# Output rows of the first block in runs of 64, one pool of two product banks, and longer planned landing times in a three-stage attention and MoE kernel

## The chip, the cores and the metric

One core of a Trainium2 chip runs the whole program: TensorE (PE) with its weight loads (PEld), VectorE (DVE), ScalarE (ACT), GpSimd (POOL) and SyncE (SP). All transfers between DRAM and SBUF are issued by SP, one after the other. The metric is the device time of one execution in microseconds, the median of several runs. TensorE's clock has two levels, 2.4 GHz (a granted clock of 1.00 in the profile) and 1.2 GHz (0.50).

## What is computed

Attention over chunks of 64 tokens, then a first network with squared ReLU, then a second one with a rational activation. All is fp32.

```python
def reference(**kwargs):                       # cut
    attn_out = _attn_ref(q, k, v)              # 8 x 8 heads, 576 tokens, head_dim 64, chunks of 64
    x = transpose(attn_out).reshape(4608, 512)
    x = _moe_ref(x, w_in, w_out)               # h = x @ w_in; r = max(h, 0); g = r*r; g @ w_out
    return _moe2_ref(x, w_in, w_out, a, b)     # d_ff = 2048 in both
def _moe2_ref(x, w_in, w_out, a, b):
    h = x @ w_in
    P = a[0] + a[1]*h + a[2]*h**2 + a[3]*h**3
    Q = 1.0 + abs(b[0])*abs(h) + abs(b[1])*h**2
    return (P / (Q + 1e-06)) @ w_out
```

## The kernel before, in words

The 4608 tokens are cut into nine blocks of 512 (NB), the 2048 hidden columns into 16 slices of 128 (NF). Each fp32 product is made of three matmuls on a high and a low part (`mm3`, L371 to L375); one such matmul of 512 columns is the unit of PE work, and twelve of them make one slice of a block.

**Stage 1** runs to about 825 us: network 1 (`mm_h` L381 for its first product, sums in the four banks `acc` for its second) with the attention of the next blocks in between. The first product of a slice goes to a PSUM bank `h`. ACT reads it with `act1` (L488, the ReLU; L489 squares it), DVE or ACT make the high part `gh`, POOL the low part `gl`. Two banks serve this, tags `h0` and `h1`, which `h_bank` (L377) hands out in turn; the same two banks also take the attention's products with v (`mm_pv2`, L582, matmul at L589; emptied by copies `ah<-h`, L199) and the transposes of the weights e (L766). A bank that was handed out can be written when the reader of its former content is through.

**Stage 2** runs from there to the end: network 2. Its first product is made for pairs of blocks by a scheme of seven products (p = 1 to 7) of six matmuls each, on sums of weights (`w2q`) and sums of x, in place of eight. A unit of this scheme (two slices, two blocks) is seven products and four jobs of the second product ("o"), about 20.4 us of PE; eight units make a block pair m = 0 to 3, so that the units are numbered 0 to 31, and the ninth block comes last. The banks are now four: `bank(i)` (L863), tags `h0`, `h1` and `b2`, `b3`, given to roles b, g, h, e of a unit by `role` (L867). The results wait there for `tile_jobs` (L1251): several operations by DVE, ACT and POOL (L922 to L970), the product `t` of POOL at L942 among them.

The sums of x for a pair are made on the side: `xq_load` (L336, DMA at L342) brings rows of x2 into a room `xroom`, `xq_sum` (L346) adds on POOL (L350), `xq_hi` (ACT) and `xq_lo` (POOL) split, `xq_store` (L362, DMA at L366) writes the pages `x2q`, which are loaded again as pages of x (L849) as the units need them. The output rows of a block leave by `store2` (L471, DMA at L476).

The order in stage 2 is set by `plan` (L1185), a list scheduler with costs and due times in units of one matmul (0.227 us). It keeps SP's queue in the order of planned starts. `X_LAT` (L1227) is how long it plans for the landing of a load of x, and also from the store of one sum to the load of the next but one into the same room. SP issues in order and can have eight transfers under way (eight semaphores in turn, DMAHW0 to DMAHW7 below): an instruction that waits holds up everything behind it on SP.

Of the kernel before, what the change touches and what calls it, by code (L numbers as in the profile page):

```python
# [9 lines left out]
F32 = mybir.dt.float32  # L10
# [6 lines left out]
PSUM = bass.MemoryType.PSUM  # L17
# [7 lines left out]
RING_O, RING_I, RING_X = 6, 12, 9  # L25
# [3 lines left out]
R_SB = "g"  # L29
MORE = 3  # L30
N_PRE = 2
TB = {"r": 3, "t": 3, "w": 3}
OF_W = {1: 0, 2: 2, 3: 7, 4: 3, 5: 4, 6: 5, 7: 6}
OF_X = {1: 0, 2: 1, 7: 2, 3: 3, 4: 4, 5: 5, 6: 6}
# [54 lines left out]
def attn_moe_moe_kernel(  # L89
# [25 lines left out]
    nc = tc.nc  # L115
    B, H, S, D = q.shape
# [4 lines left out]
    NF = DFF // 128  # L121
    NBLK = NT // NB
# [7 lines left out]
    g_p = ctx.enter_context(tc.tile_pool(name="g", bufs=3))  # L130
    r_p = ctx.enter_context(tc.tile_pool(name="r", bufs=1))
    dram_p = ctx.enter_context(tc.tile_pool(name="scr", bufs=1, space=DRAM))
    h_p = ctx.enter_context(tc.tile_pool(name="hps", bufs=1, space=PSUM))

    X = [[xs.tile([128, KC, NB], F32R, name=f"x{i}{p}") for p in range(2)] for i in range(2)]
    const = ctx.enter_context(tc.tile_pool(name="const", bufs=1))
# [22 lines left out]
    P = {}  # L159
    T = {}  # L160
# [214 lines left out]
            nc.tensor.matmul(out=o, lhsT=ah, rhs=bh, start=False, stop=last and i == len(pairs) - 1, **kw)  # L375

    def h_bank():  # L377
        T["h_n"] = T.get("h_n", 1) ^ 1
        return h_p.tile([128, 512], F32, name="h", tag=f"h{T['h_n']}")

    def mm_h(s):  # L381
        b, f = divmod(s, NF)
# [44 lines left out]
    def mm_out2(s, g):  # L427
        f = s % NF
        w = w_out(s)
        stage("out", s, 0)  # L430
        for i in range(TPB):
            gi = [x[:, i * 128:(i + 1) * 128] for x in g]
            if s < 2 * NS - 1 or i < TPB - 1:
                mm3(ACC[i], [(gi, w)], f == 0, s == 2 * NS - 2 and i == TPB - 1 or f == NF - 1)
                continue
            for j in PARTS:
                T["rest", j.start] = h_bank()
                mm3(T["rest", j.start][:, j], [(gi, [z[:, j] for z in w])], True, True)

    def g_tiles():  # L440
# [29 lines left out]

    def store2(b, i):  # L471
        t0 = b * NB + i * 128
        rows = out[t0:t0 + 128, :]
        if b == 0:
            rows = out[256 * (i // 2):256 * (i // 2) + 256, :].rearrange("(t c u) d -> c t u d", c=2, u=64)[i % 2]
        nc.sync.dma_start(out=rows, in_=T.pop(("ev", i)))  # L476

    def act1(s):
        ps = T.pop(("h", s))
# [381 lines left out]
        split_lo(nc.gpsimd, o[:, 1], o[:, 1].bitcast(F32), o[:, 0])  # L861

    def bank(i):  # L863
        i %= 4
        return h_p.tile([128, 512], F32, name="h", tag=f"h{i}") if i < 2 else P["eb"].tile([128, 512], F32, name="h", tag=f"b{i}")

    def role(un, r):  # L867
        if un == 0:
            return "bghe".index(r)
        if ("role", un, r) not in T:  # L870
            T["role", un, r] = role(un - 1, NEXT[r])
        return T["role", un, r]
# [212 lines left out]
    for t in range(NAT, NTILE + 1, 2):  # L1085
# [15 lines left out]
        u = (t - NAT) // 2  # L1101
# [79 lines left out]
    def job(eng, cost, deps, due, fn, *args):  # L1181
        jobs.append((eng, cost, deps, due, fn, args))
        return len(jobs) - 1
# [40 lines left out]
                    wait.setdefault(jobs[k][0], []).append(k)  # L1224
        return end

    E_LAT, PE_LAT, D_LAT, X_LAT = 0.6, 1.2, 13.0, 30.0  # L1227
    pe_list = []
    n_out = 0
    for m in range(NBLK // 2):  # L1230
# [50 lines left out]
    def x_jobs(i, deps):  # L1281
        m = i // 7
        if m < NBLK // 2 and ("xq", 8 * m + 7) not in made:
            later.setdefault(m, []).append((i, deps))
            return
        deps = deps + ([(made["xq", 8 * m + 7], D_LAT)] if m < NBLK // 2 else [(made["st", NBLK - 1, k], D_LAT) for k in range(KC)])
        due = nominal["p", m, 0, ORDER[i % 7]] if m < NBLK // 2 else nominal["s", 0]
        for c in range(2):
            made["x", i, c] = job("D", 6.5, deps, due - 40, xp_load, i, c)
# [6 lines left out]
    for x in pe_list:  # L1296
# [43 lines left out]
        if x[0] == "p":  # L1340
            _, m, u, p = x
            b1, b2, f0, f1 = 2 * m + 1, 2 * m, 2 * u, 2 * u + 1
            un, i = 8 * m + u, ORDER.index(p)
            j, i = 7 * un + i, 7 * m + i
            if ("i", j) in made:
                deps.append((made["i", j], D_LAT))
            if u == 0:
                deps += [(made["x", i, c], D_LAT) for c in range(2) if ("x", i, c) in made]
            if p in (1, 5):
                deps += last_of.get(role(un, "he"[p == 5]), [])  # L1350
            if p in (6, 2, 3, 7, 4):
                deps += [(made[k, un], E_LAT) for k in {6: ["fb"], 2: ["fb"], 3: ["v"], 7: ["v"], 4: ["add22"]}[p]]
            made[x] = job("PE", size["p"], deps, 0, mm_p, m, u, p)
            end = [(made[x], PE_LAT)]
            z = nominal[x]
            if j + RING_I < len(i_seq):
                i_job(j + RING_I, end)
            if u == NF // 2 - 1 and i + RING_X < 7 * (NBLK // 2) + 2:
                x_jobs(i + RING_X, end)
            if p == 1:  # L1360
                made["fb", un] = job("A", COST["cp"], end + last_of.get(role(un, "b"), []), z + 7, q_fork, un, "h", "b")
            if p == 5:
                q_ = [(made["add22", un - 1], E_LAT)] if un else []
                made["s5", un] = job("A", COST["cp"], end + q_, z + 8, q_s5)
            if p in (5, 6) and ORDER.index(p) == max(ORDER.index(5), ORDER.index(6)):
                made["v", un] = job("V", COST["add"], end + [(made["s5", un], E_LAT)], z + 8, q_v)
            if p == 2:
                last_of[role(un, "b")] = tile_jobs(b1, f0, end, z + 44, "b" not in R_SB)
            if p == 3:
                last_of[role(un, "e")] = tile_jobs(b2, f0, end, z + 44, "e" not in R_SB)  # L1370
            if p == 7:
                made["add22", un] = job("V", COST["add"], end + [(made["s5", un], E_LAT)] + last_of.get(role(un, "g"), []),
                                        z + 6, q_22, un, b2, f1)
                last_of[role(un, "g")] = tile_jobs(b2, f1, [(made["add22", un], E_LAT)], z + 44, "g" not in R_SB)
            if p == 4:
                last_of[role(un, "h")] = tile_jobs(b1, f1, end, z + 44, "h" not in R_SB)
            if u < 5 and p in (1, 7) and (u, p) != (0, 1) and m < NBLK // 2 - 1 and (m or u):
                i = 8 * m + 8 + 2 * u + (p == 7) - (1 if m else 2)
                if i < 8 * m + 16:
                    q_ = [(made["xq", i - 2], X_LAT)] if i > 9 else []  # L1380
                    e = job("D", 3, end + q_, z + 20, xq_load, i)
                    e = job("G", 10.5, [(e, X_LAT)], z + 60, xq_sum, i)
                    e = job("A", 4.3, [(e, E_LAT)], z + 75, xq_hi, i)
                    e = job("G", 10.5, [(e, E_LAT)], z + 100, xq_lo, i)
                    made["xq", i] = job("D", 11.5, [(e, E_LAT)], z + 140, xq_store, i)
                    if i == 8 * m + 15:
                        for i, q_ in later.pop(m + 1, []):
                            x_jobs(i, q_)
                        if m == 0:
                            for i in range(7, RING_X):  # L1390
                                x_jobs(i, end)
            continue
        f = x[1]
        u, i = divmod(f, 2)
# [85 lines left out]
```

## Time and profile before

| | us |
|---|---|
| median of 3 runs | 1625.17 (1623.68 to 1625.43) |
| the profiled execution | 1624.63 |
| its span, first to last instruction | 1622.9 |
| PE busy in it | 1593.5 (98%) |
| DVE, ACT, POOL busy | 1076.8, 920.5, 770.1 |
| mean granted clock of PE | 0.994 |

The profile is one execution. The sum of the prediction is made in that execution's times, and 1.7 us of it lie outside of the span. Since PE is busy 98% of the span, what matters is where it is not, and where its clock is low. The second section of the page, the span in 40 slices, has a slice in which PE falls to 7 tenths and its clock to 8: the 26th, from 1014 to 1055 us.

### The profile page before, as it was taken

Reading aid. Unit: us, or ns where it says so; the run is one execution under the profiler, and the core shown is the slowest. Engines: PE = TensorE matmul, PEld = TensorE weight load, DVE = VectorE, ACT = ScalarE, POOL = GpSimd, SP = SyncE. Lnnn points to the kernel's source line nnn. Section 1 sums busy time; section 2 is a strip of 40 time slices with the busy share of each in tenths; the row PEclk is TensorE's granted clock in tenths of the full one; section 3 lists DMA queues with packets and bytes.
Section 4 is the critical chain, followed back from the end, with each engine's and each line's share of the span. In section 5 each row is a group of like instructions: output and inputs, shape, how many; then the busy total and the mean of one; then the engine's idle time right before and its main releaser. Section 6 shows DMA issues by size and latency. Waiting matters only on the chain.

```text
span 1622.9 us, 25746 instructions
## 1 busy us (share of the span) xinstructions
PE 1593.5 (98%) x9165; PEld 1317.5 (81%) x9165; DVE 1076.8 (66%) x1688; ACT 920.5 (57%) x1462; POOL 770.1 (47%) x737
## 2 busy tenths in 40 slices
PE   8899999999999999999999999799999999999998
PEld 7778888888888888888888888688888888888887
DVE  6776676666666766653067887688788877777640
ACT  5754333333333332334578876787788778777641
POOL 3531122022221312323368864886598657555554
PEclk9999999999999999999999999899999999999999
DMA  9745575344445445544989995999999896666544
GB/s 264 215 106 137 158 239 130 86 140 107 128 115 142 119 101 144 143 124 132 318 304 296 307 346 205 305 301 304 343 292 298 299 349 213 205 210 210 179 161 138
DMA packets 359448, 337.29 MB, mean 208 GB/s; under 512 B 195352, under 2 KB 269336, under 8 KB 358296
## 3 DMA queue, kind: packets, MB, share of 16 engines
q1 hardware_dynamic: 359320, 335.64, 67.0%
q8 instruction: 73, 1.20, 0.3%
q14 instruction: 55, 0.45, 0.1%
HBM read 253.76 MB, written 81.79 MB: 207 GB/s over the span
## 4 chain that ended last, share of the span: by engine, by line
PE 91%; DVE 4%; DMA 2%; ACT 1%; issue 1%; POOL 0%; SPq 0%; DVEq 0%; ACTq 0%; POOLq 0%
PE acc L373 15%; PE acc L375 15%; PE acc L374 15%; PE h L373 15%; PE h L375 14%; PE h L374 14%; PE h L589 1%; DMA xroom<-x2d 1%; PE a L568 1%; DMA st<-in_moe_w_in_dram 1%; DVE wc L244 1%; DVE w L963 1%; DVE spare L970 0%; DMA v<-in_v_dram 0%; DVE h L967 0%
## 5 line engine op out<-in xcount | busy, mean ns | idle before, releaser
L373 PE MATMUL h<-x,w 128*128 128x512 f32 (+1 forms) x824 | 322.7, 392 | 17.9 <-DVE spare L970 9.8
L374 PE MATMUL h<-x,w 128*128 128x512 f32 (+1 forms) x824 | 321.1, 390 | 0.3 <-DVE x L202 0.3
L375 PE MATMUL h<-x,w 128*128 128x512 f32 (+1 forms) x824 | 320.9, 389 | 0.0
L942 POOL TENSOR_TENSOR t<-t,r 128x512 f32<-128x512 f32 x144 | 187.3, 1301 | 129.1 <-ACT t L934 122.3
L373 PE MATMUL acc<-gh,w 128*128 128x512 f32 x576 | 226.1, 393 | 0.0
L375 PE MATMUL acc<-gh,w 128*128 128x512 f32 x576 | 224.3, 389 | 0.0
L374 PE MATMUL acc<-gl,w 128*128 128x512 f32 x576 | 224.2, 389 | 0.0
L373 PE MATMUL acc<-w,gl 128*128 128x512 f32 x575 | 224.0, 390 | 0.0
L375 PE MATMUL acc<-w,gh 128*128 128x512 f32 x575 | 223.9, 389 | 0.0
L374 PE MATMUL acc<-w,gh 128*128 128x512 f32 x575 | 223.9, 389 | 0.0
L488 ACT ACTIVATE r<-h 128x512 f32<-128x512 f32 x124 | 74.0, 597 | 255.6 <-PE h L375 159.1
L202 POOL TENSOR_TENSOR gl<-spare,gh 128x512 fp32r<-128x512 f32 x146 | 192.3, 1322 | 50.7 <-ACT gh L197 45.6
L199 POOL CAST st<-wc 128x512 fp32r<-128x512 f32 x32 | 21.2, 663 | 375.7 <-DVE wc L244 337.0
L373 PEld LDWEIGHTS h<-x,w 128*128 128x128 f32 x824 | 155.8, 189 | 51.9 <-DVE spare L970 10.3
L374 PEld LDWEIGHTS h<-x,w 128*128 128x128 f32 x824 | 156.0, 189 | 32.2 <-DVE x L202 0.5
L375 PEld LDWEIGHTS h<-x,w 128*128 128x128 f32 x824 | 156.0, 189 | 32.1
L199 DVE CAST gh<-r 128x512 fp32r<-128x512 f32 x117 | 58.0, 496 | 149.0 <-ACT r L489 148.3
L946 DVE TENSOR_TENSOR w<-w,h 128x512 f32<-128x512 f32 x144 | 98.3, 683 | 66.8 <-ACT w L938 66.8
L963 DVE SCALAR_TENSOR_TENSOR w<-w,co,h 128x512 f32<-128x512 f32 x112 | 83.4, 745 | 67.0 <-ACT h L959 67.0
L373 PEld LDWEIGHTS acc<-gh,w 128*128 128x128 f32 x576 | 108.2, 188 | 23.1
L373 PEld LDWEIGHTS acc<-w,gl 128*128 128x128 f32 x575 | 108.3, 188 | 22.5
L375 PEld LDWEIGHTS acc<-gh,w 128*128 128x128 f32 x576 | 108.1, 188 | 22.6
(145 smaller groups left out, 3083.2 us busy)
## 6 DMA issues: line engine op xcount, KB each, us to landing
w<-w2o SPq DMA_DIRECT2D x144, 512.0 KB, 4.7
w<-w2q SPq DMA_DIRECT2D x256, 256.0 KB, 4.9
x2q<-xroom SPq DMA_DIRECT2D x24, 896.0 KB, 6.6
st<-in_moe_w_in_dram SPq DMA_DIRECT2D x32, 512.0 KB, 4.8
st<-in_moe_w_out_dram SPq DMA_DIRECT2D x32, 512.0 KB, 4.7
w2q<-st SPq DMA_DIRECT2D x32, 512.0 KB, 2.9
w<-x2q SPq DMA_DIRECT2D x30, 512.0 KB, 7.3
x<-x2q SPq DMA_DIRECT2D x26, 512.0 KB, 7.6
```

What stands on the lines that cost most here:

```text
L199: eng.tensor_copy(out=o, in_=x)
L202: eng.tensor_tensor(out=o, in0=x, in1=hi.bitcast(F32), op=ALU.subtract)
L244: nc.vector.scalar_tensor_tensor(out=c, in0=c, scalar=3, in1=st[:, :, 0], op0=ALU.logical_shift_left, op1=ALU.bitwise_or)
L373: nc.tensor.matmul(out=o, lhsT=al, rhs=bh, start=first and i == 0, stop=False, **kw)
L374: nc.tensor.matmul(out=o, lhsT=ah, rhs=bl, start=False, stop=False, **kw)
L375: nc.tensor.matmul(out=o, lhsT=ah, rhs=bh, start=False, stop=last and i == len(pairs) - 1, **kw)
L488: nc.scalar.activation(out=r, in_=ps, func=ACTF.Relu)
L568: nc.tensor.matmul(out=o[half(c), h, p], lhsT=q_[half(h), p, half(c)], rhs=k_[half(h), p, half(c)], start=True, stop=True)
L589: nc.tensor.matmul(out=o[c][half(h), i, p], lhsT=v_[half(c), 2 * p + h], rhs=a_[h][half(c), p] if t < 2 * TPB else a_[h][half(c), :, p], s ...
L942: nc.gpsimd.tensor_tensor(out=t, in0=t, in1=T["r", b, f], op=ALU.mult)
L946: nc.vector.tensor_tensor(out=w, in0=w, in1=T["H", b, f], op=ALU.mult)
L963: nc.vector.scalar_tensor_tensor(out=w, in0=w, scalar=co[:, 0:1], in1=T["r", b, f], op0=ALU.add, op1=ALU.mult)
```

## The change

Three edits.

1. The PSUM pool of the first product has one tag, `h`, with two buffers, in place of two tags of one buffer each. `h_bank` asks for the next buffer of that tag; the pool gives the one that is released first in the order of the program. In stage 2 `bank` takes each of its four tiles once and keeps it.
2. `store2` writes the rows of block 0 in two transfers of 64 rows each, where one transfer with an outer dimension of two wrote all 128 (rows of two different places in DRAM, since block 0's tokens are paired by 64).
3. `X_LAT` is 42 where it was 30. `X_AT` writes the former condition on which unit and product start a sum of x in another form; it is met at the same places.

```diff
-    h_p = ctx.enter_context(tc.tile_pool(name="hps", bufs=1, space=PSUM))
+    h_p = ctx.enter_context(tc.tile_pool(name="hps", bufs=2, space=PSUM))
     def h_bank():
-        T["h_n"] = T.get("h_n", 1) ^ 1
-        return h_p.tile([128, 512], F32, name="h", tag=f"h{T['h_n']}")
+        return h_p.tile([128, 512], F32, name="h", tag="h")
...
-                T["rest", j.start] = h_bank()
+                T["rest", j.start] = bank(role(NF // 2 * (NBLK // 2) - 1, "be"[j.start > 0]))
...
     def store2(b, i):
         t0 = b * NB + i * 128
-        rows = out[t0:t0 + 128, :]
-        if b == 0:
-            rows = out[256 * (i // 2):256 * (i // 2) + 256, :].rearrange("(t c u) d -> c t u d", c=2, u=64)[i % 2]
-        nc.sync.dma_start(out=rows, in_=T.pop(("ev", i)))
+        ev = T.pop(("ev", i))
+        if b:
+            nc.sync.dma_start(out=out[t0:t0 + 128, :], in_=ev)
+            return
+        for t in range(2):
+            r0 = 256 * (i // 2) + 128 * t + 64 * (i % 2)
+            nc.sync.dma_start(out=out[r0:r0 + 64, :], in_=ev[64 * t:64 * t + 64])
...
     def bank(i):
-        i %= 4
-        return h_p.tile([128, 512], F32, name="h", tag=f"h{i}") if i < 2 else P["eb"].tile([128, 512], F32, name="h", tag=f"b{i}")
+        if ("bank", i) not in T:
+            T["bank", i] = h_bank() if i < 2 else P["eb"].tile([128, 512], F32, name="h", tag=f"b{i}")
+        return T["bank", i]
...
-    E_LAT, PE_LAT, D_LAT, X_LAT = 0.6, 1.2, 13.0, 30.0
+    E_LAT, PE_LAT, D_LAT, X_LAT = 0.6, 1.2, 13.0, 42.0
...
-            if u < 5 and p in (1, 7) and (u, p) != (0, 1) and m < NBLK // 2 - 1 and (m or u):
-                i = 8 * m + 8 + 2 * u + (p == 7) - (1 if m else 2)
-                if i < 8 * m + 16:
-                    q_ = [(made["xq", i - 2], X_LAT)] if i > 9 else []
+            if p in (1, 7) and m < NBLK // 2 - 1 and 2 * u + (p == 7) in X_AT[m > 0]:
+                i = 8 * m + 8 + X_AT[m > 0].index(2 * u + (p == 7))
+                q_ = [(made["xq", i - 2], X_LAT)] if i > 9 else []
```

On PE no instruction moves; some of its waits name other engines. In stage 1, with `acc3` the last sums of the slice before and `h_1104` the first product of the next slice (`w0` are weights, `x00` and `x01` the block's two parts), before:

```order
L375 MATMUL acc3_583<-gh_958,w1_4_92 128x512
L373 MATMUL h_1104<-x00_69,w0_8_84 128x512 [waits DVE_49,Activation_49,Pool_49]
L374 MATMUL h_1104<-x01_70,w0_8_84 128x512
L375 MATMUL h_1104<-x00_69,w0_8_84 128x512
L373 MATMUL h_1104<-x00_69,w0_8_84 128x512
```

and now:

```order
L376 MATMUL acc3_583<-gh_958,w1_4_92 128x512
L374 MATMUL h_1104<-x00_69,w0_8_84 128x512 [waits Activation_49]
L375 MATMUL h_1104<-x01_70,w0_8_84 128x512
L376 MATMUL h_1104<-x00_69,w0_8_84 128x512
L374 MATMUL h_1104<-x00_69,w0_8_84 128x512
```

The tile `h_1104` now takes the bank whose last reader is an ACT instruction (the ReLU of the tile `h_1039`) instead of the one that a DVE copy `ah<-h` empties. Two slices on, around `h_1382`, there are twelve matmuls of the product and then the transposes of e; before, the last of them are:

```order
L375 MATMUL h_1382<-x00_69,w0_11_87 128x512
L766 MATMUL h_1401<-ident_143,e_1311 128x128 [waits Activation_49]
L766 MATMUL h_1401<-ident_143,e_1311 128x128 x3
L373 MATMUL acc0_580<-gh_1275,w1_8_94 128x512 [waits Pool_49]
L374 MATMUL acc0_580<-gl_1276,w1_8_94 128x512
```

and now:

```order
L376 MATMUL h_1382<-x00_69,w0_11_87 128x512
L769 MATMUL h_1401<-ident_143,e_1311 128x128 [waits DVE_49,PE_49]
L769 MATMUL h_1401<-ident_143,e_1311 128x128 x3
L374 MATMUL acc0_580<-gh_1275,w1_8_94 128x512 [waits Pool_49]
L375 MATMUL acc0_580<-gl_1276,w1_8_94 128x512
```

The first matmul of `h_1382` waited for DVE and ACT and now waits for ACT alone; the wait for DVE's copy has moved twelve matmuls down, to the transposes. On SP, in the second block pair where block 0's rows are stored (`out_0_dram<-ev`) and the second row group of x is loaded (`xroom1`), before:

```order
L342 DMA xroom0_8056<-x2d2_97 128x4x128 [waits DMAHW5_49]
L831 DMA w0_0_76<-w2q2_118 128x512 [waits DMAHW6_49,PE_49]
L274 DMA w1_2_8284<-w2o2_110 128x1024 [waits DMAHW7_49,PE_49]
L831 DMA w0_1_77<-w2q2_118 128x512 [waits DMAHW0_49,PE_49]
L476 DMA out_0_dram<-ev_10045 2x64x512 [waits DMAHW1_49,Activation_49]
L476 DMA out_0_dram<-ev_10051 2x64x512 [waits DMAHW2_49,DVE_49]
L476 DMA out_0_dram<-ev_10053 2x64x512 [waits DMAHW3_49,Activation_49]
L476 DMA out_0_dram<-ev_10065 2x64x512 [waits DMAHW4_49,DVE_49]
L342 DMA xroom1_8057<-x2d2_97 128x4x128 [waits DMAHW5_49]
L274 DMA w1_2_8284<-w2o2_110 128x1024 [waits DMAHW6_49,PE_49]
```

and now:

```order
L275 DMA w1_0_8262<-w2o1_109 128x1024 [waits DMAHW2_49,PE_49]
L479 DMA out_0_dram<-ev_10006 64x512 [waits DMAHW3_49,Activation_49]
L479 DMA out_0_dram<-ev_10006 64x512 [waits DMAHW4_49]
L479 DMA out_0_dram<-ev_10012 64x512 [waits DMAHW5_49,DVE_49]
L479 DMA out_0_dram<-ev_10012 64x512 [waits DMAHW6_49]
L479 DMA out_0_dram<-ev_10014 64x512 [waits DMAHW7_49,Activation_49]
L479 DMA out_0_dram<-ev_10014 64x512 [waits DMAHW0_49]
L479 DMA out_0_dram<-ev_10026 64x512 [waits DMAHW1_49,DVE_49]
L479 DMA out_0_dram<-ev_10026 64x512 [waits DMAHW2_49]
L343 DMA xroom1_8057<-x2d2_97 128x4x128 [waits DMAHW3_49]
L834 DMA w0_5_81<-w2q2_118 128x512 [waits DMAHW4_49]
L275 DMA w1_2_8284<-w2o2_110 128x1024 [waits DMAHW5_49,PE_49]
```

Four stores have become eight, and they stand some weight loads earlier: the loads of `w0_5` and `w0_0` from `w2q2`, which stood ahead of the stores, now stand behind them. The load of `xroom1` is the next transfer behind the stores in both. On POOL, around that room's sum (`xroom1`, L350, now L351), with `t` the operation L942 (now L946) of the tiles, before:

```order
L199 CAST gh_10153<-spare1_8010 128x512 [waits PE_49]
L202 TENSOR_TENSOR gl_10154<-spare1_8010,gh_10153 128x512 [waits Pool_49]
L350 TENSOR_TENSOR xroom1_8057<-xroom1_8057 128x128 [waits DMAHW5_49,DMAHW1_49]
...
L942 TENSOR_TENSOR t_10156<-t_10156,r_10150 128x512 [waits DVE_49,Activation_49]
L942 TENSOR_TENSOR t_10189<-t_10189,r_10185 128x512 [waits DVE_49,Activation_49]
L202 TENSOR_TENSOR gl_10175<-spare1_8010,gh_10174 128x512 [waits PE_49]
```

and now:

```order
L946 TENSOR_TENSOR t_10119<-t_10119,r_10115 128x512 [waits DVE_49,Activation_49]
L203 TENSOR_TENSOR gl_10100<-spare1_8010,gh_10099 128x512 [waits Pool_49]
L351 TENSOR_TENSOR xroom1_8057<-xroom1_8057 128x128 [waits DMAHW3_49]
...
L946 TENSOR_TENSOR t_10168<-t_10168,r_10165 128x512 [waits DVE_49,Activation_49]
L203 TENSOR_TENSOR gl_10134<-spare1_8010,gh_10133 128x512 [waits PE_49]
```

Before, two `t` stood right behind the sum; now the first of them stands ahead of it. The sums of x of the three pairs move too: the last store of a pair's sums stands on SP behind 62, 114 and 170 weight loads of `w2q` where it stood behind 54, 108 and 164, and the 14 loads of x pages for the second block pair (L849), of which four stood behind 56 or 57 such loads and ten behind 61 or 62, stand in one run behind 64.

## Rows read from the trace of the kernel before

**Rows 1.** Waits of PE: engine, line, releaser: us in total, times, longest

```profile
PE h L373 <- DVE spare L970: 9.8, 1, 9.8
PE h L373 <- DVE ah L199: 7.4, 2, 3.8
```

**Rows 2.** Timeline of PE, 66 to 112: start, us, instruction [idle before <-releaser]

```profile
68.08 0.39 PE L373 MATMUL acc<-gh,w 128*128 128x512 f32 x1
...
70.58 0.39 PE L375 MATMUL acc<-gh,w 128*128 128x512 f32 x1
74.81 0.77 PE L373 MATMUL h<-x,w 128*128 128x512 f32 x1 [3.84 <-DVE ah L199]
...
99.96 0.47 PE L373 MATMUL h<-x,w 128*128 128x512 f32 x1 [3.52 <-DVE ah L199]
```

**Rows 3.** Timeline of DVE in those stretches, 66 to 76 and 94 to 101

```profile
74.23 0.43 DVE L199 COPY ah<-h 64x256 f32<-64x256 f32 x1
...
98.95 0.87 DVE L199 COPY ah<-h 64x256 f32<-64x256 f32 x2
```

**Rows 4.** Timeline of ACT in the same stretches

```profile
68.34 0.60 ACT L488 ACTIVATE r<-h 128x512 f32<-128x512 f32 x1 [0.81 <-PE h L375]
...
95.00 0.58 ACT L488 ACTIVATE r<-h 128x512 f32<-128x512 f32 x1
```

**Rows 5.** Timeline of POOL, 66 to 76

```profile
68.57 4.48 POOL L202 TENSOR_TENSOR w<-wc,w 128x512 fp32r<-128x512 f32 x3
```

**Rows 6.** Windows: us, PE, PEld, DVE, ACT, POOL busy (x), PE clock, DMA share, GB/s

```profile
74.81:80.06 5.25, 5.25 (x12) 4.10 (x13) 0.57 (x1) 0.00 (x0) 0.00 (x0) 0.50 0.18 28
96.45:99.96 3.51, 0.00 (x0) 0.03 (x1) 3.37 (x7) 1.56 (x3) 1.86 (x3) 1.00 0.66 172
99.96:104.38 4.42, 4.42 (x13) 3.43 (x14) 0.92 (x2) 0.00 (x0) 1.28 (x1) 0.61 0.04 7
994.00:1003.00 9.00, 9.00 (x41) 7.46 (x40) 8.79 (x10) 6.48 (x10) 7.01 (x8) 1.00 0.15 52
1024.88:1029.04 4.16, 4.16 (x10) 3.33 (x11) 4.05 (x7) 3.68 (x7) 3.89 (x4) 0.50 0.99 307
960.00:980.00 20.00, 20.00 (x90) 16.55 (x89) 14.53 (x22) 15.27 (x24) 11.07 (x10) 1.00 1.03 393
```

**Rows 7.** Timeline of PE, 953 to 1031: second block pair

```profile
974.08 0.39 PE L373 MATMUL h<-x,w 128*128 128x512 f32 x1
...
1024.88 0.80 PE L373 MATMUL h<-x,w 128*128 128x512 f32 x1 [9.84 <-DVE spare L970]
```

**Rows 8.** Chain of what ended last, 985 to 1030: start, us, step

```profile
1003.19 14.88 DMA xroom<-x2d
1018.20 0.46 POOL xroom L350
...
1020.01 1.24 POOL t L942
```

**Rows 9.** Timeline of SP, 930 to 1110: start, us, issues

```profile
955.60 0.58 SPq L831 DMA_DIRECT2D w<-w2q  x1
...
959.99 6.44 SPq L849 DMA_DIRECT2D w<-x2q  x6
...
993.26 9.88 SPq L476 DMA_DIRECT2D out_dram<-ev  x4
1003.19 4.96 SPq L342 DMA_DIRECT2D xroom<-x2d  x1
```

**Rows 10.** DMA issues of the whole span: count, KB each, median us to landing

```profile
x<-x2q SPq DMA_DIRECT2D x26, 512.0 KB, 7.6
...
out_dram<-ev SPq DMA_DIRECT2D x35, 256.0 KB, 3.9
...
xroom<-x2d SPq DMA_DIRECT2D x24, 256.0 KB, 4.7
...
v<-in_v_dram SPq DMA_DIRECT2D x16, 128.0 KB, 5.6
```

More of the change, by code (lines that the diff above doesn't have):

```diff
@@ L31 @@
 N_PRE = 2
+X_AT = (2, 3, 4, 5, 6, 7, 8, 9), (1, 2, 3, 4, 5, 6, 7, 8)
 TB = {"r": 3, "t": 3, "w": 3}
@@ L1376, in attn_moe_moe_kernel @@
                 last_of[role(un, "h")] = tile_jobs(b1, f1, end, z + 44, "h" not in R_SB)
-            if u < 5 and p in (1, 7) and (u, p) != (0, 1) and m < NBLK // 2 - 1 and (m or u):
-                i = 8 * m + 8 + 2 * u + (p == 7) - (1 if m else 2)
-                if i < 8 * m + 16:
-                    q_ = [(made["xq", i - 2], X_LAT)] if i > 9 else []
[L1381 to L1391, printed above, removed]
+            if p in (1, 7) and m < NBLK // 2 - 1 and 2 * u + (p == 7) in X_AT[m > 0]:
+                i = 8 * m + 8 + X_AT[m > 0].index(2 * u + (p == 7))
+                q_ = [(made["xq", i - 2], X_LAT)] if i > 9 else []
+                e = job("D", 3, end + q_, z + 20, xq_load, i)
+                e = job("G", 10.5, [(e, X_LAT)], z + 60, xq_sum, i)
+                e = job("A", 4.3, [(e, E_LAT)], z + 75, xq_hi, i)
+                e = job("G", 10.5, [(e, E_LAT)], z + 100, xq_lo, i)
+                made["xq", i] = job("D", 11.5, [(e, E_LAT)], z + 140, xq_store, i)
+                if i == 8 * m + 15:
+                    for i, q_ in later.pop(m + 1, []):
+                        x_jobs(i, q_)
+                    if m == 0:
+                        for i in range(7, RING_X):
+                            x_jobs(i, end)
             continue
```

## The prediction, made before the changed kernel ran

> **What bounds the kernel now.** I read the table first: PE is busy 1593.5 of 1622.9 us, so that only 29.4 us without PE work can be won at all, and whatever the clock costs on top. Next the waits of PE: one wait of 9.8 us for DVE's L970 and two that make 7.4 us for the copies `ah<-h` of L199 [rows 1]; all others are at most 1.4 us. The timeline of PE gives the places: 3.84 us before 74.81 and 3.52 us before 99.96, both in stage 1 at the first product of a slice [rows 2], and 9.84 us before 1024.88, in unit 10 of stage 2 [rows 7]. Call them A, B and C. Together they are 17.2 of the 29.4 us. Then the windows, for the clock behind each: after A twelve matmuls take 5.25 us at 0.50, after B twelve take 4.42 us at 0.61, after C the clock is 0.50 for 4.16 us [rows 6]. At full clock one matmul is a step of 0.227 us (2.50 us for the eleven steps from 68.08 to 70.58 [rows 2]), so twelve are 2.72 us, and the low clock costs 2.53 us after A, 1.70 us after B, and half of 4.16, about 2.0 us, after C. In each of the three the clock was low only once PE had been idle; I count it as lost with the wait.
>
> **The bank pool, at A.** PE's order stays. Before, the first matmul of `h_1104` waited for the bank that DVE empties; that copy ran from 74.23 to 74.66 [rows 3], behind other work on a busy DVE, and PE began at 74.81. Now it takes the other bank, whose last reader is the ReLU of `h_1039`: 68.34 to 68.94 on ACT [rows 4]. PE is done with the slice before at 70.97 (74.81 less 3.84), two us later, so nothing is left to wait for there. Its weights: the second half of the twelve needs a low part from POOL, the first of three that run from 68.57 for 4.48 us [rows 5], so done at about 70.1, needed at 70.97 + 6 x 0.227 = 72.3. The wait for the copy does not vanish, it passes to the product with v, which stands behind these twelve and twelve more sums: PE is there at 70.97 + 24 x 0.227 = 76.4, after 74.66. What is next late? In the window 74.81 to 80.06 ACT and POOL do nothing, DVE 0.57 us, and the DMA share is 0.18 [rows 6]: all of them waited for PE and can come earlier with it. So A gives 3.84 + 2.53 = **6.37 us**. The least it can give is 0 (if the loads of this stage turn out to run by their own time), the most is 6.37.
>
> **The bank pool, at B.** The same exchange: `h_1382` takes the bank of the ReLU that ran 95.00 to 95.58 [rows 4], and PE is free at 96.44. But the wait for the copies, which end at 98.95 + 0.87 = 99.82 [rows 3], now stands only twelve matmuls further on, at the transposes of e. PE gets there at 96.44 + 2.72 = 99.16, so 0.66 us stay as a wait. DVE is the limit in that stretch, 3.37 of 3.51 us busy [rows 6], and doesn't come earlier. B gives 3.52 + 1.70 - 0.66 = **4.56 us**; between 3.5 (the short wait costs clock too, as much as itself) and 5.2.
>
> After B everything in stage 1 comes earlier by the sum of both, 10.9 us. ACT has no work in the window behind B either, and the DMA share is 0.04 [rows 6]; I find no second stall of this kind in PE's waits, so nothing more to take away, and I put down nothing for new ones (up to 1 us for transfers that had just been in time).
>
> **The stores, at C.** The chain of waits into 1024.88 is short: a load of `xroom` issued at 1003.19 needs 14.88 us; POOL stands at its sum (L350) until 1018.20; behind that sum stands the product `t` (1020.01), and from there it is 4.9 us through ACT and DVE to PE [rows 7, 8]. Such a load needs 4.7 us as a rule [rows 10]. What is ahead of it on SP are the four stores of block 0, issued from 993.26 in 9.88 us [rows 9]. During 994 to 1003 the DMA share is 0.15 with 52 GB/s, and a window earlier in the pair, 960 to 980, has 1.03 with 393 GB/s [rows 6]: with eight transfers under way at most, four of which move slowly on some two of sixteen engines, everything behind them is held up. Other stores of a block, 128 rows in a single run, land in 3.9 us [rows 10]. The only difference is the leading dimension of two.
>
> With 64 rows in one run a store should use many engines. No row shows such a store; the nearest are 3.9 us for the 128-row store and 5.6 us for loads of v of the same 128 KB in smaller pieces [rows 10]. I take the 3.9, since the rows are equally long, and the 5.6 as the other end. The load of `xroom` must land for POOL by 1015.04 - 4.9 - 1.8 (1020.01 less 1018.20) = 1008.3 to cost nothing even with the old order on POOL. Issued at 1003.19 as before and landing in 4.7 us it is there at 1007.9; with no slow store in the eight places it is issued earlier. Besides, POOL's order has changed as well: one `t` that stood behind the sum now stands before it, so that the tile which PE wants no longer hangs on the load. Two reasons, each enough. C gives 9.84 + 2.0 = **11.84 us**.
>
> On this the Trainium skill, "DMA: Bandwidth & Descriptors", section "Rules for kernel authors", has a rule that speaks against the edit: two transfers to disjoint halves of the partitions are not worth it, since "they serialize". The same section says that an outermost dimension of c < 16 confines a transfer to c engines; by that rule the halves gain far more here than they lose, and the 0.15 agrees with it. The first rule compares with one transfer that uses all engines, which the old store is not; what serializing would give is the second rival below.
>
> Four more issues on SP at 0.3 to 0.6 us [rows 9] are 1.2 to 2.4 us of SP's time, at a place where it waited 9.88 us: nothing. SP now comes to the stores some weight loads earlier and waits there for the output to be copied out of PSUM (about 993). What is queued behind are weight loads of unit 10, wanted at 1015: over 15 us of slack. If that were gone, PE would wait for weights as long as a load takes, 5 us.
>
> **The longer landing time.** The sums of x end later by 6 to 8 weight loads, 2.9 us each (seven in a unit of 20.4 us): 17 to 23 us. The pages of the second pair are loaded in one run. In the old time the 62nd weight load was issued at 955.60 [rows 9], so the 64th comes at about 961.4, and the 14 pages follow at 1.07 us each (six in 6.44 us [rows 9]), the last at 976. With 7.6 us to land [rows 10] the first two pages are there by 971, needed at 974.08 [rows 7], and the last by 984, needed by the unit's seventh product, 72 matmuls in, at 990.4. The gain of this edit for the path is nothing by itself: no wait of PE for pages shows in the list [rows 1]. Its side effect is the POOL order at C. X_AT and `rest` cost nothing.
>
> **The sum.** 6.37 + 4.56 + 11.84 = 22.8 us. Against the profiled execution: 1624.63 - 22.8 = 1601.9. The median of the runs is 0.5 higher, so **1602** for the median. With B at its lower end and 1 us lost to late transfers it is 1604.5; with B at its upper end and some of the small waits gone 1599.
>
> **The rivals.**
> *C stays, the stores are slow still.* If 64 rows go to a few engines as well, and POOL's order doesn't help: A and B alone, 1624.6 - 10.9 = 1613.7. For it: no row of a 64-row store. Against: the 128-row stores, and the loads of v. 4 in 100.
> *The halves go one after the other.* Eight stores at half of 3.9 us each from 993.3 end at 1008.9, the load of `xroom` lands at 1013.6; with the old order on POOL PE would start 6.7 us later, at 1020.3, 5.3 us too late, with some 2 us of clock behind it: of C 4.5 us are won, 1624.6 - 10.9 - 4.5 = 1609. For it: nothing on the rows shows how short stores share engines. Against: POOL's order. 5 in 100. (This is the first rule of the Trainium skill cited above.)
> *The banks don't pay.* Stage 1 might run by DVE or by its loads, and the wait move on: C alone, 1612.8. For it: DVE is 3.37 of 3.51 us busy at B, and a wait of 0.66 us is already in sight. Against: all other engines are empty right after both waits. 7 in 100.
> *Pages late at the first change of pair.* If the load of pages, in one run at a DMA share above 1, needs 14.88 us like the load of `xroom` did, the first two land at 977, 3 us late, and with the clock behind it, as after A, 5 to 7 us are given back: 1608. 10 in 100.
> *Slower.* The sums of x are 17 to 23 us later at every change of pair (m = 0, 1, 2); if they had no such slack, PE would wait for pages at all three. To end slower by over 0.2% (3.3 us, about what a measurement of this kernel can tell from no change) it takes 22.8 + 3.3 = 26.1 us, so 8.7 us with its clock at each: then 1628 and above. For it: no view of before shows how early the pages were. Against: the weight loads that pace the move are the units' own, and at the first change the margin comes to 3 us or more. 5 in 100, and 3 in 100 for about even.
>
> **How the numbers follow.** The forecast, 1599 to 1605, has 66 in 100, late pages 10, stores in turn 5, C unchanged 4, banks without gain 7, about even 3, slower 5. Faster by over 0.2%: 92 in 100. The range runs from 1599 to 1611, which takes in the forecast, the late pages and the stores in turn, some 80 in 100.
>
> **What would show it.** At A no wait before the first product, clock 1.00 behind it. At B a wait of some 0.7 us that has moved to L769, releaser DVE L199. At C eight stores in SP's list, a DMA share well above 0.15 behind them, the `xroom` load at about 5 us, no wait for L970. A wait of PE for pages at the first change of pair (974 less the 10.9, so 963), or at all three (163 us apart), would show the late pages or the slower case; the stalls A and B under another line's name, the banks that don't pay. The prediction fails above all if a wait that these three cover now comes up behind them.

## The result

| | before | changed |
|---|---|---|
| median | 1625.3 us (1623.68 to 1625.99, 4 runs) | 1602.44 us (1602.02 to 1602.69, 4 runs) |
| span of the profiled execution | 1622.9 us | 1600.4 us |
| PE busy in it | 1593.5 us | 1587.4 us |
| mean granted clock | 0.994 | 1.000 |

The ratio is 0.986, 95% interval [0.9843, 0.9878]: 22.9 us less, where 22.8 were forecast. PE's time without work in the span went from 29.4 to 13.0 us. Its busy time, for the same 9165 matmuls at a mean clock of 1.000, is the other 6 us shorter.

The waits of PE in the changed kernel (engine, line, releaser: us in total, times, longest), against [rows 1]:

```profile
PE a L408 <- POOL ident masks.py:199: 1.4, 1, 1.4
PE a L740 <- DMA v<-in_v_dram: 1.2, 1, 1.2
PE h L374 <- DVE h L926: 1.0, 2, 0.8
PE h L769 <- DVE ah L200: 0.8, 1, 0.8
```

Both long entries are gone. What stays of them is the fourth row: the wait for the copies `ah<-h`, moved to the transposes at L769.

The timeline of PE at the places A and B, against [rows 2]:

```profile
70.78 0.39 PE L376 MATMUL acc<-gh,w 128*128 128x512 f32 x1
71.01 0.39 PE L374 MATMUL h<-x,w 128*128 128x512 f32 x1
...
92.39 0.39 PE L376 MATMUL h<-x,w 128*128 128x512 f32 x1
93.59 0.63 PE L769 MATMUL h<-ident,e 128*128 128x128 f32 x4 [0.82 <-DVE ah L200]
```

At A the first product follows the last sum after 0.23 us, one step. At B the twelve matmuls run through, and PE stands 0.82 us behind them. Windows there and in unit 10 (us, busy time and instructions of PE, PEld, DVE, ACT, POOL, PE's clock, DMA share, GB/s), against [rows 6]:

```profile
70.97:73.70 2.73, 2.73 (x13) 2.26 (x13) 2.73 (x3) 2.20 (x4) 2.19 (x2) 1.00 1.07 401
89.90:92.77 2.87, 2.87 (x13) 2.06 (x11) 2.78 (x5) 1.85 (x3) 2.04 (x3) 1.00 0.40 73
93.59:98.00 4.41, 4.41 (x22) 3.72 (x23) 4.05 (x6) 2.46 (x4) 2.12 (x1) 1.00 0.48 103
983.00:992.00 9.00, 9.00 (x41) 7.45 (x40) 8.75 (x12) 6.87 (x12) 5.44 (x7) 1.00 0.77 186
1003.00:1020.00 17.00, 17.00 (x77) 14.08 (x76) 13.14 (x20) 13.65 (x23) 11.92 (x11) 1.00 0.98 323
```

The clock is 1.00 in each; behind the short wait of 0.82 us too. While block 0 is stored (983 to 992) the DMA share is 0.77, where it was 0.15. Unit 10 begins at about 1004 without a gap. SP's timeline in the changed kernel, against [rows 9]:

```profile
950.39 4.69 SPq L852 DMA_DIRECT2D x<-x2q  x8
955.99 6.98 SPq L852 DMA_DIRECT2D w<-x2q  x6
...
983.17 5.31 SPq L479 DMA_DIRECT2D out_dram<-ev  x8
988.52 0.60 SPq L343 DMA_DIRECT2D xroom<-x2d  x1
```

and the DMA issues in 980 to 1000 (count, KB each, median us to landing), against [rows 10]:

```profile
out_dram<-ev SPq DMA_DIRECT2D x8, 128.0 KB, 2.4
...
xroom<-x2d SPq DMA_DIRECT2D x1, 256.0 KB, 3.0
```

Eight stores are issued in 5.31 us and land in 2.4 us each. The load of `xroom` right behind them is issued in 0.60 us and lands 3.0 us after its issue began, where it took 14.88. The pages of x begin at 950.39; the prediction had 961.4 less the 10.9 us won before, 950.5.

### The profile page after: what moved, and what is told of

Same layout as the page of the kernel before. It is cut to its first block, busy times and chain, and to the rows that moved or that the text cites. A ratio compares the mean times of both kernels' runs of the same rounds, so it can differ in the third digit from the quotient of the medians.

```text
span 1600.4 us, 25717 instructions
## 1 busy us (share of the span) xinstructions
PE 1587.4 (99%) x9165; PEld 1313.8 (82%) x9165; DVE 1075.1 (67%) x1688; ACT 921.6 (58%) x1462; POOL 772.7 (48%) x737
## 4 chain that ended last, share of the span: by engine, by line
PE 94%; DVE 3%; SPq 1%; ACT 1%; DMA 0%; issue 0%; POOL 0%; DVEq 0%; POOLq 0%; ACTq 0%
PE acc L374 16%; PE acc L376 16%; PE acc L375 16%; PE h L374 15%; PE h L376 15%; PE h L375 15%; PE h L592 1%; PE a L571 1%; DVE w L967 1%; SPq L662 1%; DVE spare L974 0%; DMA qn<-in_q_dram 0%; DVE w L954 0%; DVE w L950 0%; DVE h L971 0%
## 5 line engine op out<-in xcount | busy, mean ns | idle before, releaser
L946 POOL TENSOR_TENSOR t<-t,r 128x512 f32<-128x512 f32 x144 | 188.3, 1308 | 135.1 <-ACT t L938 129.9
L203 POOL TENSOR_TENSOR gl<-spare,gh 128x512 fp32r<-128x512 f32 x146 | 191.3, 1316 | 54.3 <-ACT gh L198 48.2
L950 DVE TENSOR_TENSOR w<-w,h 128x512 f32<-128x512 f32 x144 | 98.4, 683 | 67.1 <-ACT w L942 64.3
L376 PEld LDWEIGHTS acc<-w,gh 128*128 128x128 f32 x575 | 107.9, 188 | 22.5
```

Source lines behind the costliest of these rows:

```text
L203: eng.tensor_tensor(out=o, in0=x, in1=hi.bitcast(F32), op=ALU.subtract)
L946: nc.gpsimd.tensor_tensor(out=t, in0=t, in1=T["r", b, f], op=ALU.mult)
L950: nc.vector.tensor_tensor(out=w, in0=w, in1=T["H", b, f], op=ALU.mult)
```

## The experiments

Two theories were to be told apart at each place. At A and B: the bank was all that PE waited for, or DVE and the loads bound the stage and the wait only moves. At C: the slow stores, the order on POOL, or both, made the stall; and for edit 3, whether it gives or costs anything.

**Edit 1 alone** (pool of two banks, kept tiles in stage 2).

```diff
-    h_p = ctx.enter_context(tc.tile_pool(name="hps", bufs=1, space=PSUM))
+    h_p = ctx.enter_context(tc.tile_pool(name="hps", bufs=2, space=PSUM))
... (cut: the other lines of edit 1)
```

> Edit 1 alone (the pool of two banks, persistent tiles in stage 2); stores and landing time as before. Theory: A (6.4 us) and B (4.6 us) go, C stays with its 9.8 us wait for L970 and 2 us of clock: 10.9 us less, ratio 0.993, and a short wait of 0.7 to 0.8 us at the transposes of e (DVE L199). Rival (the banks don't pay, stage 1 runs by DVE or its loads): ratio 1.000, with A and B under other names.

Ratio 0.9946 [0.9933, 0.996], 1614.54 us; span 1612.7, 10.2 us less than before. Its waits of PE:

```profile
PE h L374 <- DVE spare L971: 10.0, 1, 10.0
...
PE h L766 <- DVE ah L200: 0.8, 1, 0.8
```

A and B are gone, C is there whole, the short wait is at the transposes. By the times it is 8.8 us (6.5 to 10.9), by the spans of the two traced executions 10.2, for a forecast of 10.9. Executions of one kernel differ by some 4 us (the kernel before ran from 1621.34 to 1625.76 us beside this one), so the stretch itself tells more: from the transposes of e ahead of A to those behind B it was 39.49 us before (64.89 to 104.38) and is 28.50 now (65.06 to 93.56), 11.0 less. The rival, nothing, is out.

**Stall A alone, stall B alone.** In each run one stall is taken away and the other left: the old alternation with one step left out, at the tile of A (the 19th bank taken) or at that of B (the 25th).

```diff
-        T["h_n"] = T.get("h_n", 1) ^ 1
+        T["h_c"] = T.get("h_c", -1) + 1
+        T["h_n"] = T.get("h_n", 1) ^ (T["h_c"] == 18) ^ 1      # A; 24 for B
```

> The kernel before, in which the alternation of the two banks skips one step at the tile of stall A alone, so that it takes the bank of the ReLU; B and C stay. Theory: 6.4 us less (3.84 of wait, 2.5 of clock), ratio 0.9961, next 74 us without a new wait, B still 3.5 us under DVE L199. Rival (the clock after A would be low anyway, or the time goes to the next stage): 3.8 us less or nothing, ratio 0.9976 to 1.000.

> The kernel before, in which the alternation of the two banks skips one step at the tile of stall B alone; A and C stay. Theory: the 3.52 us wait goes, 0.7 to 0.8 us come back at the transposes, and the clock behind (1.7 us) is won: 4.5 us less, ratio 0.9972. Rival (DVE bounds that stretch, the wait only moves): 1 us or less, ratio 0.9994 or above.

Without A: ratio 0.9966 [0.9953, 0.9978], 5.5 us (3.6 to 7.6), span 6.5 us less. Without B: ratio 0.9968 [0.9956, 0.9981], 5.2 us (3.1 to 7.2), span 5.1 us less, 0.6 of it because the wait at C was 9.2 us in that execution. PE's timeline with the transposes ahead of A, between A and B and behind B, first of the kernel before, then of the one without A (the wait shown is its only one between 68 and 104), then of the one without B:

```profile
64.89 0.60 PE L766 MATMUL h<-ident,e 128*128 128x128 f32 x4
...
90.31 0.66 PE L766 MATMUL h<-ident,e 128*128 128x128 f32 x4
...
104.38 0.60 PE L766 MATMUL h<-ident,e 128*128 128x128 f32 x4
```

```profile
65.38 0.60 PE L767 MATMUL h<-ident,e 128*128 128x128 f32 x4
...
84.20 0.66 PE L767 MATMUL h<-ident,e 128*128 128x128 f32 x4
...
93.85 0.62 PE L373 MATMUL h<-x,w 128*128 128x512 f32 x1 [3.51 <-DVE ah L199]
```

```profile
75.07 0.47 PE L373 MATMUL h<-x,w 128*128 128x512 f32 x1 [3.72 <-DVE ah L199]
...
89.72 0.66 PE L767 MATMUL h<-ident,e 128*128 128x128 f32 x4
...
99.39 0.63 PE L767 MATMUL h<-ident,e 128*128 128x128 f32 x4 [0.83 <-DVE ah L199]
```

Each stall goes without the other, and the pool isn't needed for it: what counts is which bank the one tile takes. The 3.51 us of B stay as they were after A is gone, so nothing of A was given back there. That the clock counts with the wait is told by the stretch around A: from one group of transposes to the next it was 25.42 us and is 18.82 without A, 6.6 less for a wait of 3.84. The stretch around B was 14.07 us and is 9.67 without B, 4.4 less. The times alone don't show the clock's part at A: their 3.6 to 7.6 us take in the rival's 3.8.

**Edit 2 alone** (block 0 stored by 64 rows).

```diff
-            rows = out[256 * (i // 2):256 * (i // 2) + 256, :].rearrange("(t c u) d -> c t u d", c=2, u=64)[i % 2]
... (cut: the rest of edit 2)
+            r0 = 256 * (i // 2) + 128 * t + 64 * (i % 2)
+            nc.sync.dma_start(out=out[r0:r0 + 64, :], in_=ev[64 * t:64 * t + 64])
```

> Edit 2 alone (block 0 stored by 64 rows). POOL's order at C is that of before: the sum of x stands ahead of the product t that PE wants. Theory (slow stores are the cause of C by themselves): the load of xroom takes about 5 us, C goes, 11.8 us less, ratio 0.9927; A and B stay. Rival (the halves go one after the other): the load lands about 6 us late, 5 us of C stay, 4 to 5 us less, ratio 0.997. Rival (64 rows are as slow): ratio 1.000, load 14 us or more.

Ratio 0.9927 [0.9915, 0.994], 1612.16 us: 11.9 us less, for a forecast of 11.84. SP's timeline, and then POOL's:

```profile
993.17 5.28 SPq L479 DMA_DIRECT2D out_dram<-ev  x8
998.50 0.60 SPq L342 DMA_DIRECT2D xroom<-x2d  x1
```

```profile
1004.74 1.85 POOL L350 TENSOR_TENSOR xroom<-xroom 128x128 f32<-128x128 f32 x4
1006.55 1.29 POOL L945 TENSOR_TENSOR t<-t,r 128x512 f32<-128x512 f32 x1
```

The old order on POOL stays, the sum ahead of `t`, and the sum runs at 1004.74 at once, with no wait for its load. The stores are enough by themselves.

**Edit 3 alone** (planned landing time 42; the stores strided as before).

```diff
-    E_LAT, PE_LAT, D_LAT, X_LAT = 0.6, 1.2, 13.0, 30.0
+    E_LAT, PE_LAT, D_LAT, X_LAT = 0.6, 1.2, 13.0, 42.0
```

> Edit 3 alone (planned landing time 42); the stores of block 0 stay strided, so the load of xroom behind them stays near 15 us. Now t stands ahead of that sum on POOL. Theory as predicted (POOL's new order alone is enough): C goes, ratio 0.9927. Rival: the slow stores hold the loads and the sum all the same, and the next tile behind the sum, or a weight load behind the stores, is late instead: a wait of 4 to 10 us of PE stays in unit 10, ratio 0.996 to 1.000.

Ratio 0.9985 [0.9976, 0.9993], 2.4 us less, where 11.8 were forecast if the order on POOL were enough. The prediction's second reason falls. SP's, POOL's and PE's timelines of this kernel, and a window of it, in this order:

```profile
994.70 9.73 SPq L476 DMA_DIRECT2D out_dram<-ev  x4
1004.47 4.95 SPq L342 DMA_DIRECT2D xroom<-x2d  x1
```

```profile
1018.87 1.82 POOL L350 TENSOR_TENSOR xroom<-xroom 128x128 f32<-128x128 f32 x4 [9.54 <-DMA xroom<-x2d]
```

```profile
1019.59 0.56 PE L373 MATMUL h<-x,w 128*128 128x512 f32 x1 [3.11 <-DMA w<-w2q]
...
1023.21 0.79 PE L373 MATMUL acc<-w,gl 128*128 128x512 f32 x1 [0.92 <-POOL gl L202]
```

```profile
1019.59:1027.00 7.41, 6.49 (x16) 4.63 (x17) 3.39 (x5) 5.56 (x8) 7.41 (x9) 0.54 0.97 309
```

The tile that PE wanted no longer hangs on the sum, and the wait for L970 is gone. But the weight load `w2q` that unit 10 wants stands on SP behind the same slow stores. PE waits 3.11 us for it, 0.92 us more for a low part of POOL at 1023.21, and runs at a clock of 0.54 from 1019.59 to 1027: about 3 us of its 6.5 busy. That is some 7 of the 11.8 us of C. Another 1.7 us of waiting for DVE L922 comes between 1060 and 1110. The reordering only chose who stands behind the stores.

**Edits 1 and 2 without 3**, on two chips, and **the changed kernel again** beside it on the second.

```diff
-    E_LAT, PE_LAT, D_LAT, X_LAT = 0.6, 1.2, 13.0, 42.0
+    E_LAT, PE_LAT, D_LAT, X_LAT = 0.6, 1.2, 13.0, 30.0
```

> Edits 1 and 2 without edit 3 (landing time 30). Theory: A, B and C all go without it, and it adds nothing by itself: ratio to before 0.986, the same as the changed kernel within 0.1%. Rival (the longer landing time carries part of C): a wait of PE of 2 us or more left in unit 10, ratio 0.988 or above.

> Edits 1 and 2 without edit 3, again, beside the changed kernel: ratio to before 0.986, within 0.1% of it by the theory that edit 3 adds nothing once the stores are fast.

> The changed kernel again, beside the next one on one chip. Ratio to before 0.986. Theory: the longer landing time adds nothing, so it lies within 0.1% of the next kernel. Rival: the small waits of the tiles in stage 2 that its trace has (1.0 us for DVE h L926) make it slower by 0.1% or more.

Without edit 3: 0.9866 [0.9853, 0.9879] and 0.9863 [0.985, 0.9877], 1602.46 us the second time. With it, beside that: 0.9862 [0.9846, 0.9877], 1602.79 us. Edit 3 is worth nothing that shows, once the stores are fast; the intervals leave room for some 2 us either way. The waits for L926 that the changed kernel has beside the one without edit 3, 1.0 us in all, are within what single executions differ by at the start: the trace of the second run without edit 3 has 4.5 us of waits for loads of v, nearly all within the first 33 us, where the changed kernel has 1.2.

**Full stores in place of halves.** This kernel leaves out the pairing of block 0's tokens by 64: its rows go to other places in the output, in four stores of 128 rows.

```diff
-        for t in range(2):
-            r0 = 256 * (i // 2) + 128 * t + 64 * (i % 2)
-            nc.sync.dma_start(out=out[r0:r0 + 64, :], in_=ev[64 * t:64 * t + 64])
... (cut)
+        nc.sync.dma_start(out=out[t0:t0 + 128, :], in_=T.pop(("ev", i)))
```

> The changed kernel, but block 0's rows stored in one run of 128 per tile, four stores in place of eight (the rows go to other places in the output: the pairing by 64 is left out). It tells what the halves cost against one full transfer. Theory (16 engines either way, nothing on PE's path): time as the changed kernel, ratio to before 0.986 within 0.1%; a full store lands in about 3.5 to 4 us, a half in 2.4, four issues take about half of the 5.31 us. Rival (halves go one after the other and cost the load behind them): the load of xroom lands earlier by several us; on the time still nothing.

Ratio 0.9867 [0.9852, 0.9882], as the changed kernel. SP's timeline and then the DMA issues of 980 to 1000:

```profile
984.03 2.46 SPq L473 DMA_DIRECT2D out_dram<-ev  x4
986.54 0.53 SPq L343 DMA_DIRECT2D xroom<-x2d  x1
```

```profile
out_dram<-ev SPq DMA_DIRECT2D x4, 256.0 KB, 3.5
...
xroom<-x2d SPq DMA_DIRECT2D x1, 256.0 KB, 3.6
```

A full store lands in 3.5 us, a half in 2.4. The halves cost what the second issue costs, 2.85 us of SP for four more. The load behind them takes no longer from its own issue (3.0 against 3.6 us), but counted from the first store it lands after 8.3 us, against 6.1 here: so much of the rival holds, and on the time it is nothing, as the rival said too. What was slow was the leading dimension of two, not the transfer's size and not the number of transfers.

**The slow stores issued by ACT** in place of SP, all else as before.

```diff
-        nc.sync.dma_start(out=rows, in_=T.pop(("ev", i)))
+        (nc.sync if b else nc.scalar).dma_start(out=rows, in_=T.pop(("ev", i)))
```

> The kernel before, with the four strided stores of block 0 issued by ACT instead of SP: as slow as before, but they hold none of SP's eight places. Theory 'places' (C comes from SP standing behind the slow stores): the load of xroom is issued about 993, lands in about 5 us, C goes, ratio 0.9927. Theory 'engines' (the load's own share on the two busy engines waits behind the stores' packets): the load still takes 10 us or more, PE waits 5 to 10 us in unit 10, ratio 0.996 to 1.000.

Ratio 0.999 [0.9981, 0.9999], in the range of the theory of engines, but PE's wait comes by a way that neither theory had. SP's timeline, ACT's with its own issues (ACTq), PE's, and the DMA issues at 990.82 and 994.89 (count, KB, us to landing):

```profile
991.18 0.53 SPq L342 DMA_DIRECT2D xroom<-x2d  x1
```

```profile
992.13 1.14 ACTq L476 DMA_DIRECT2D out_dram<-ev  x1
...
994.05 5.87 ACTq L476 DMA_DIRECT2D out_dram<-ev  x1
999.97 0.72 ACT L959 ACTIVATE r<-r,co 128x512 f32<-128x512 f32 x1 [5.27 <-issue]
1000.04 6.41 ACTq L476 DMA_DIRECT2D out_dram<-ev  x1
1006.50 0.58 ACT L197 ACTIVATE h<-h 128x512 f32<-128x512 f32 x1 [5.81 <-issue]
```

```profile
1007.14 0.80 PE L373 MATMUL h<-x,w 128*128 128x512 f32 x1 [8.19 <-ACT h L197]
```

```profile
w<-w2q SPq DMA_DIRECT2D x1, 256.0 KB, 3.1
...
w<-w2q SPq DMA_DIRECT2D x1, 256.0 KB, 7.4
```

C did not go, since the stores hold whoever issues them. The first two are issued in 1.14 and 0.53 us, the third and fourth keep ACT for 5.87 and 6.41 us, and PE then waits 8.19 us for ACT. The last of the four outputs was in SBUF by 994.23 (DVE's copy `ev<-acc` of 993.54), so at 1000.04 ACT had nothing else to wait for. Before, SP stood in a like way: of the 9.88 us for the four stores 8.37 went to the third and fourth, and 4.96 to the issue of the load behind them [rows 9].

The run does not tell the two theories apart. The load of `xroom` landed in 3.8 us, but it was issued at 991.18, ahead of the first store at 992.13. Loads that SP issued behind the first stores were slow, though SP did not issue the stores: a load of `w2q` took 7.4 us (issued at 994.89) where one of the same size, ahead of the stores, took 3.1 (at 990.82). As far as this pair of loads can show, the stores slow the loads beside them as well, as the theory of engines said, if by less than its 10 us.

**A landing time of 60.**

```diff
-    E_LAT, PE_LAT, D_LAT, X_LAT = 0.6, 1.2, 13.0, 42.0
+    E_LAT, PE_LAT, D_LAT, X_LAT = 0.6, 1.2, 13.0, 60.0
```

> The changed kernel with a planned landing time of 60 in place of 42: the pages of x stand 4 weight loads (11.6 us) later on SP at the first change of pair, 8 and 7 (some 20 us) at the others. It tells how much room the move had. Theory (room of 5 us at the first change, about 16 at the others): PE waits for pages some 6, 7 and 4 us at the three changes, with clock behind each: 1615 to 1630 us, ratio 0.993 to 1.003. Rival (the pages are never late, as the weight loads pace them): 1602 us, ratio 0.986.

Ratio 1.0072 [1.0058, 1.0086]: slower than before the change, 33 us slower than with 42, above the range of the theory. The waits of PE, and SP's timeline at the first change of pair:

```profile
PE h L374 <- DVE w L950: 12.9, 2, 6.8
PE h L374 <- DMA x<-x2q: 12.7, 2, 11.9
```

```profile
968.33 0.37 SPq L367 DMA_DIRECT2D x2q<-xroom  x1
968.75 8.23 SPq L852 DMA_DIRECT2D x<-x2q  x8
```

At the first change the pages are issued at 968.75, 18.4 us later than with 42, not 11.6: the last store of the sums now stands right ahead of them, and is late itself. PE waits 11.87 us from 963.04. At the two other changes PE waits 6.12 and 6.80 us for DVE L950. Ahead of the first of these, from 1120 to 1143, POOL is busy 22.2 of 23 us and DVE 19.3, with the last sums of x among POOL's work; that the sums make the wait was not tried by itself, and it was not foreseen. The waits make 25.6 us; PE is also busy 7.9 us longer than in the changed kernel (1595.3 against 1587.4), at a mean clock of 0.991. So later pages can cost as the slower rival had it, and 42 lies between two values of which the lower is as good and the higher loses everything.

**The short wait at B.** Two of the copies on ACT, with edits 1 and 2 and the old landing time.

```diff
... (lines cut, figures rounded)
-    "cp611": 'V',
+    "cp610": 'A', "cp611": 'A',
-    "f_copy:6,1,0": 0.079, "f_copy:6,1,1": 0.08,
+    "f_copy:6,1,0": 0.479, "f_copy:6,1,1": 0.48,
```

> Edits 1 and 2 with the old landing time, and two of the three DVE copies of attention weights at place B done by ACT, which has 2.4 us of idle time there. Theory (the short wait left at B is DVE's own work, two copies of 0.87 us in all): the 0.8 us wait at the transposes goes, nothing else moves: 0.8 us less than the same kernel without it, 0.05%, at the edge of what timing shows, so the trace decides. Rival (DVE's softmax multiply, 1.75 us, ends as late): the wait stays above 0.5 us under another releaser.

1602.59 us, where the same kernel without it had 1602.46 on that chip. Window from 40 to 100, first of this kernel, then of the one without:

```profile
40.00:100.00 60.00, 60.00 (x423) 49.18 (x422) 53.02 (x80) 46.42 (x83) 34.29 (x28) 1.00 0.73 191
```

```profile
40.00:100.00 60.00, 59.17 (x419) 48.45 (x418) 52.88 (x82) 46.57 (x83) 37.11 (x30) 1.00 0.76 205
```

PE has no idle time left there: the 0.8 us went, as the theory had it. In the total it doesn't show, and its trace has a wait of 1.8 us for a weight split on POOL (L203) further on, which the changed kernel's second trace has as well, with 1.4 us, and its first has not. None of the versions beats the changed kernel by more than its runs differ.

## Why the prediction was right, and where it was not

**A.** Forecast 6.37 us, measured alone 6.6 us by the stretch of PE's timeline and 5.5 us (3.6 to 7.6) by the times. The wait that passes to the product with v shows nowhere, as worked out.

**B.** Forecast 4.56 us, measured alone 4.4 us by the stretch, 5.2 us (3.1 to 7.2) by the times. The rest of the wait was put at 0.66 us and is 0.82 us; the clock stayed at 1.00 behind it, so the case of the lower bound, that the short wait costs clock too, did not come. (That bound, 3.5, does not follow from its own words: 4.56 less another 0.66 is 3.9. Nothing hangs on it.) That it is DVE's own work is shown by the copies on ACT, with which it goes.

**C.** Forecast 11.84 us, measured alone 11.9 us. The figure is right, but one step of its working is wrong: "Two reasons, each enough." The stores are enough. The new order on POOL is not: alone it left some 7 us, because the weight loads stand behind the same stores. The prediction looked at the queue behind the stores for the new kernel, where the stores are fast, and didn't ask the same for the order alone with the stores slow. In the sum the step had no weight, since both came together.

**How the slow stores hold the rest up** was told as eight places of which four move slowly, with everything behind them held up. The trace of before does not bear out the places: the load's own place, DMAHW5, was last used by the load of `xroom0` at 986.88, which landed in 4.2 us, 12 us before SP came to the load behind the stores. What it shows is two other holds. The issue itself stands: 8.37 us for the third and fourth store, 4.96 for the load, and on ACT 5.87 and 6.41 us for the third and fourth store. And a load is slow once issued: this one landed 9.9 us after its issue was through, and beside the stores of ACT a load took 7.4 us in place of 3.1. How the 14.88 us divide between the two by cause, and what in the chip makes the issue stand, was not taken apart; it stays open. The size of C didn't hang on it, since it was read from PE's wait and its clock.

**The two rules** of the Trainium skill, "DMA: Bandwidth & Descriptors", section "Rules for kernel authors": that a leading dimension below 16 confines a transfer to at most that many engines agrees with the runs. With the strided stores on ACT, a queue that carries those four stores alone (1.05 MB) kept 13.0% of the 16 engines' time busy from 1003.3 to 1005, which is two engines. With 64 or 128 rows leading, a store lands in 2.4 or 3.5 us, and with the halves the DMA share is 0.77 in place of 0.15. That two halves serialize, so that one should use a full transfer, is not contradicted: four full stores were issued in less than half the time, and the load behind them landed 2.2 us sooner after the first store. For the time of the kernel it did not matter.

**Edit 3** was costed at nothing, which the two runs beside one another bear out (0.9862 with, 0.9863 without). The margin of the first pages was worked out as 3 us. The run at 60 puts it higher: with the pages 18.4 us later PE waited 11.87 us, so some 6 us were left with 42. The chance of 5 in 100 for the slower rival was for this kind of loss; with 60 it came to 33 us, 11 a change on average, where the rival needed 8.7, but at two of the three it came by way of DVE's work and not by pages.

**The sum.** By the times of each alone: A 5.5, B 5.2, C 11.9, together 22.6 us, against 22.9 us for all. Each of these has an interval of some 2 us either way, and A and B in one run gave 8.8, so the close agreement of the total is in part luck. That the parts add up rests better on the stretches, 6.6 and 4.4 us, and on the 11.0 for both in the run of edit 1.

## What to carry to other kernels

On an engine that is busy 98% of the time, list every wait and read the clock behind each: the three here were 17.2 us of waiting and cost 22.9. When a wait is for a buffer, look which instruction empties it; another buffer whose reader is long through may be had without more memory. Look at the leading dimension of a transfer: one with two was dearer here than two with 64, and moving other work around it only changed who stood behind it.

## What the hardware showed that was not expected

The issue of a strided store, 256 KB with a leading dimension of two, is quick for the first two (1.14 and 0.53 us on ACT) and keeps the issuing engine for 5.87 and 6.41 us from the third on; stores of the same bytes with a leading dimension of 128 are issued in 2.46 us for four. So such a transfer is not only late itself, it stops the engine that hands it over, compute included when that engine is ACT (idle for 5.27 and 5.81 us behind the two issues). A load that another engine issued was slow beside it too: 256 KB by SP, beside the stores of ACT, took 7.4 us, where the same size ahead of them took 3.1.
